# Fused attention and MLP: first tokens normalized in two pairs, a bank of its own for each first sum, and new constants for the instruction plan

## The chip, the cores and the metric

One core of a Trainium2 chip runs the whole kernel. The metric is device microseconds (us) of one execution. The kernel before takes 823.89 us, the median of three runs (822.95 to 825.45). A profiled execution gives a span, 1.8 to 2.0 us shorter than the timed value of the same execution; the accounts below are accounts of spans.

## The reference, cut to what matters

`x` is 2048 x 512, bf16. All three outputs are added.

```python
xn = _layernorm(x, axis=-1)
return x + _A_ref(xn, A_wqkv, A_wo) + _B_ref(xn, B_w1, B_b1, B_w2, B_b2)
# _A_ref: 32 heads of 16
#   p = softmax(q k^T / 4); o = p v; o @ wo
# _B_ref: gelu(layernorm(x) @ w1 + b1) @ w2 + b2, 512 -> 1792 -> 512
```

Attention needs 32 x 2048 x 2048 exponentials, and they decide the time.

## The kernel before

The kernel is a program that plans a program. Each piece of work is added as an operation with an engine, an estimated duration, a priority, its dependences and the PSUM bank that it takes or gives back. A list scheduler simulates the engines with those durations, and the order that it finds becomes the fixed order of instructions on each engine. On the chip every engine works through its list in order and waits by semaphore. So a constant that moves one operation can re-order everything after it; I call each outcome a **plan**.

Queries are worked in groups of 4 heads x 512 queries. For each of 16 key tiles (128 keys) a group needs four **units**: the scores of one head, 128 x 512, in one PSUM bank. ScalarE takes the exponentials of most tiles, two or three units to an instruction. VectorE takes the rest by an int16 bit trick: four conversions from PSUM and four shifted adds for each tile, followed by 20 value products on TensorE where ScalarE's tiles need 4. Value products go into an accumulator bank; at the end of a group the sum is copied out, its denominators travel through DRAM and come back as a broadcast (`rlb`), and VectorE multiplies.

The constants, and the pool of banks for the very first sums:

```python
    early = _Pool([res[7], res[4]])
    wide = _Pool([res[i] for i in (7, 5, 4, 3, 2, 1, 0)])
    T0, KG = 15.0, 15.5
    OUT0, OUT1 = 0.475, 0.25
    OUT, OPEN, RES, RESL, SLK, ALP = 3, 1, 20, 24, 40.0, 25.0
    KTP, QTP = 70.0, 70.0
    HOT = 1
    XACT = 2
    RATE, QO, PO, AO, DO = 23.75, 55.0, 39.5, 25.0, 17.0
```

`OPEN` is how many key tiles may be open for VectorE at once, `RES` how many units must be left in a group for VectorE to be given another of its tiles; `QO`, `AO`, `DO` are offsets of the priorities of query sums, shifted adds and VectorE's value products.

Normalization of four tokens' tiles, with one GpSimd power for all four:

```python
        sl = slice(4 * g, 4 * g + 4)
        ...
        def frs():
            I(nc.gpsimd.tensor_scalar(out=wv1[:, sl], in0=mv[:, sl, 1], scalar1=LN_EPS, ...))
            I(nc.gpsimd.tensor_tensor(out=r1[:, sl], in0=wv1[:, sl], in1=mhalf[:, sl],
                                      op=ALU.pow))
        r = add("POOL", 0.9, frs, [st_op[t] for t in tt] + [mk_half], pr)
        pool = early if g else wide
```

The value products of ScalarE's tile `k` wait for the values of `k`, and also for those of tile `k + 1`; this will matter:

```python
        deps = [unit_exp[g, k, j] for k in ks for j in range(HS)]
        deps += [va_op[k] for k in ks] + [va_op[min(k + 1, NT - 1)] for k in ks]
```

The planner also keeps TensorE's clock up. Where the plan leaves a gap and the last 3.4 us hold less than `NEED` of planned work (in units of 0.215 us), it puts in matmuls of zeros ("fills"):

```python
    NEED = 9.5
    ...
                if (t1 - t0 < 2.0
                        and sum(d for (a, d) in log[-40:] if a > t - 3.4) >= NEED):
                    t += 0.1
                    continue
```

## Time and profile before

| what | us | how to read it |
|---|---|---|
| span of the profiled execution | 820.5 | this execution was timed at 822.46 |
| first exponential | 14.77 | the start: load, normalize, project |
| ScalarE busy from first to last exponential | 777.6 | "work" |
| ScalarE idle in that stretch, before 100 us | 5.8 | "early holes" |
| the same, after 100 us | 10.7 | "late holes" |
| after the last exponential | 11.6 | "tail": last group, output |

These five add up to the span (to rounding), because ScalarE's exponentials run from 14.77 to 808.89. TensorE (94%) and VectorE (90%) are nearly as busy as ScalarE (95%). The lines themselves are in the prediction.

### The profile page before, as it was taken

How to read it: one execution, taken by the hardware profiler on the slowest of the kernel's cores; microseconds unless marked ns; L12 is line 12 of the kernel's file. 1: busy time of each engine (PE TensorE's matmuls, PEld its weight loads, DVE VectorE, ACT ScalarE, POOL GpSimd, SP SyncE). 2: the span in 40 equal slices, each digit the busy share in tenths (PEclk: the TensorE clock that was granted, in tenths of full speed). 3: DMA queues.
4: the chain of work that ended last, by engine and by line, in shares of the span. 5: the costliest groups of instructions: out<-in, count | busy, mean ns of one | idle time of the engine just before them, and what ended most of it. 6: DMA issues, size and time to landing. Idle time of an engine off the chain costs nothing.

```text
span 820.5 us, 22781 instructions
## 1 busy us (share of the span) xinstructions
PE 774.9 (94%) x9671; PEld 256.7 (31%) x9672; DVE 736.4 (90%) x1273; ACT 782.4 (95%) x682; POOL 54.8 (7%) x163
## 2 busy tenths in 40 slices
PE   7999899999999999999999999999999999999997
PEld 3333223333333333233322333323322332333233
DVE  7858999996899998978899998898899999998996
ACT  4899999999999999999999999999999999999994
POOL 2300000000000000000000000000000100000001
PEclk9999999999999999999999999999999999999999
DMA  5400121201100112000001012100001021100010
GB/s 180 116 4 2 34 45 38 49 13 29 29 17 21 48 34 54 27 17 15 9 23 33 30 48 61 28 2 22 22 16 34 27 56 41 29 22 21 4 32 32
DMA packets 54796, 27.96 MB, mean 34 GB/s; under 512 B 40613, under 2 KB 50598, under 8 KB 54690
## 3 DMA queue, kind: packets, MB, share of 16 engines
q1 hardware_dynamic: 52818, 25.03, 11.2%
q8 instruction: 76, 1.25, 0.7%
q10 hardware_dynamic: 1872, 1.44, 0.6%
q14 instruction: 30, 0.25, 0.1%
HBM read 23.85 MB, written 2.61 MB: 32 GB/s over the span
## 4 chain that ended last, share of the span: by engine, by line
PE 38%; DVE 33%; ACT 15%; issue 8%; DMA 6%; POOL 0%; SPq 0%; DVEq 0%; ACTq 0%
ACT p_sb L1197 14%; PE ps L597 14%; DVE x_sb L1274 13%; PE ps L1050 12%; PE ps L1032 11%; DVE tb_x L1299 7%; DVE x_sb L1299 4%; DMA rlb<-rdram 4%; DVE ht L1454 2%; DMA rdram<-rc 1%; DVE stats L719 1%; DVE osb L1333 1%; DVE ont L1347 1%; DVE vs L923 1%; DMA ldram<-osb 1%
## 5 line engine op out<-in xcount | busy, mean ns | idle before, releaser
L1197 ACT ACTIVATE p_sb<-ps 128x1024 bf16<-128x1024 f32 (+1 forms) x656 | 741.6, 1245 | 17.4 <-PE ps L1032 11.5
L1032 PE MATMUL ps<-qz,kt 32*128 32x512 bf16 x2048 | 316.4, 382 | 27.7 <-DVE x_sb L1274 10.5
L1274 DVE TENSOR_SCALAR x_sb<-ps 128x512 int16<-128x512 f32 x440 | 291.6, 683 | 15.4 <-PE ps L1032 14.1
L1299 DVE TENSOR_SCALAR tb_x<-x_sb 128x2048 int16<-128x2048 int16 x293 | 197.0, 684 | 3.5 <-PE ps L1050 2.5
L1032 PEld LDWEIGHTS <-kt 32*128 32x128 bf16 x2048 | 85.5, 91 | 281.1 <-issue 275.0
L1050 PE MATMUL ps<-p_sb,va 128*32 128x512 bf16 x1608 | 158.6, 389 | 0.2 <-DVE x_sb L1274 0.2
L1050 PE MATMUL ps<-tb_x,vs 128*32 128x512 f16 x1172 | 108.5, 382 | 1.1 <-DVE tb_x L1299 0.6
L1299 DVE TENSOR_SCALAR x_sb<-x_sb 128x2048 int16<-128x2048 int16 x147 | 100.4, 683 | 2.8 <-PE ps L1050 2.2
L1050 PEld LDWEIGHTS <-va 128*32 128x32 bf16 x2048 | 48.2, 93 | 109.0 <-issue 106.8
L1050 PEld LDWEIGHTS <-vs 128*32 128x32 bf16 x1760 | 48.1, 95 | 49.1 <-issue 30.5
L1354 POOL TENSOR_SCALAR okt<-lc 128x16 f32<-128x16 f32 x31 | 13.2, 427 | 711.9 <-DMA lc<-ldram 711.9
L597 PE MATMUL ps<-yT,w_r 128*32 128x512 bf16 x896 | 58.6, 381 | 1.3 <-DVE ht L1454 0.6
L597 PE MATMUL ps<-w_sb,ht 128*32 128x512 bf16 x896 | 59.8, 380 | 0.0
L1050 PE MATMUL ps<-x_sb,vs 128*32 128x512 f16 x588 | 57.9, 382 | 1.0 <-DVE x_sb L1299 0.7
L1454 DVE TENSOR_SCALAR ht<-ps,b_sb 128x512 bf16<-128x512 f32 x56 | 41.6, 744 | 6.1 <-PE ps L597 6.1
L1050 PE MATMUL ps<-x_sb,va 128*32 128x512 f16 x440 | 43.3, 383 | 1.2 <-DVE x_sb L1274 0.8
L597 PE MATMUL ps<-wo_pad,ont 128*32 128x512 bf16 x512 | 34.2, 381 | 1.1 <-DVE x_sb L1274 0.6
L597 PEld LDWEIGHTS <-w_r 128*32 128x32 bf16 x896 | 21.6, 96 | 25.3 <-issue 12.1
L1347 DVE TENSOR_TENSOR ont<-osb,rlb 128x512 bf16<-128x512 f32 x31 | 21.3, 687 | 8.4 <-DMA rlb<-rdram 8.4
L1333 DVE COPY osb<-ps 128x512 f32<-128x512 f32 x31 | 21.2, 683 | 8.4 <-PE ps L1050 8.4
L597 PEld LDWEIGHTS <-ht 128*32 128x32 bf16 x896 | 21.7, 96 | 21.1 <-issue 5.9
L1464 ACT ACTIVATE ht<-ht 128x3584 bf16<-128x3584 bf16 x8 | 25.1, 3182 | 0.0
(100 smaller groups left out, 360.2 us busy)
## 6 DMA issues: line engine op xcount, KB each, us to landing
rlb<-rdram SPq DMA_DIRECT2D x31, 256.0 KB
w_r<-in_B_w_dram SPq DMA_DIRECT2D x56, 128.0 KB
x_r<-in_A_x_dram SPq DMA_DIRECT2D x16, 128.0 KB
w_sb<-in_B_w_dram SPq DMA_DIRECT2D x1, 1792.0 KB
out_dram<-ot SPq DMA_DIRECT2D x12, 128.0 KB
x_sb<-in_A_x_dram SPq DMA_DIRECT2D x2, 512.0 KB
wkv<-in_A_wqkv_dram ACTq DMA_DIRECT2D x1, 512.0 KB
x_sb<-in_A_x_dram ACTq DMA_DIRECT2D x1, 512.0 KB
```

Of the source, the lines that this page charges most:

```text
L597: I(nc.tensor.matmul(dst[32 * j:32 * j + 32], lhsT=lhsT[:, 32 * j:32 * j + 32], rhs=rhs, start=start, stop=stop, tile_position=(0, 32 * j)))
L719: I(nc.vector.bn_stats(out=stats[:, t, :], in_=x_sb[:, t, :]))
L1032: I(nc.tensor.matmul(ps[:, bank, :], lhsT=kt[lo:lo + 32, s // 2, k * P:(k + 1) * P], rhs=qz[lo:lo + 32, (qt * NB + s // 2) % NQB, s % 2, : ...
L1050: I(nc.tensor.matmul(ps[32 * j:32 * j + 32, o_bank[g], :], lhsT=vals[:, h * VS:h * VS + 32], rhs=wts(j), start=pv_done[g] == 1, stop=end, ...
L1197: I(nc.scalar.activation(p_sb[:, s0:s1, :].rearrange("p a b -> p (a b)"), ps[:, b0:b0 + n, :].rearrange("p a b -> p (a b)"), AF.Exp, scale ...
L1274: I(nc.vector.tensor_scalar(out=ib[sl][:, j, :], in0=ps[:, pool.bank(key), :], scalar1=LEVEL, scalar2=0.0, op0=ALU.add, op1=ALU.max))
L1299: I(nc.vector.tensor_scalar(out=tb[x % NTB].rearrange("p j q -> p (j q)"), in0=ib[sl].rearrange("p j q -> p (j q)"), scalar1=float(SHIFT[t ...
L1333: e0 = add("DVE", dve(QW), lambda: I(nc.vector.tensor_copy(osb[:, i2, :], ps[:, o_bank[g], :])), pvs + before, pr - 1000, rel=(o_done(g),))
L1347: e4 = add("DVE", dve(QW), lambda: I(nc.vector.tensor_tensor(out=ont[:, slot, :], in0=osb[:, i2, :], in1=rlb[:], op=ALU.mult)), [e3] + lis ...
L1354: I(nc.gpsimd.tensor_scalar(out=okt[:, 0, :], in0=lc[:, i2, :], scalar1=L_MIN, scalar2=None, op0=ALU.is_ge))
L1454: I(nc.vector.tensor_scalar(out=ht[:, fc, :], in0=ps[:, misc.bank(key), :], scalar1=b1_sb[:, fc:fc + 1], scalar2=None, op0=ALU.add))
L1464: I(nc.scalar.activation(out=hv, in_=hv, func=AF.Gelu_apprx_tanh, scale=1.0))
```

## The change

The intent: start the exponentials sooner, give ScalarE less to do, and let the planner keep more VectorE tiles in flight. The diff, cut to its core:

```diff
-    wide = _Pool([res[i] for i in (7, 5, 4, 3, 2, 1, 0)])
+    wide = {key: _Pool([res[i]]) for key, i in (
+        (("xt", 0), 0), (("xt", 1), 1), (("xt", 2), 2), (("xt", 3), 3),
+        (("k", 0, 0), 7), (("k", 0, 1), 7), (("q", 0, 0), 4))}
-    T0, KG = 15.0, 15.5
-    OUT0, OUT1 = 0.475, 0.25
+    T0, NST = 14.0, 12.3
+    KG, R0, VSP, NFI = 15.5, 29.0, 400.0, 2
+    VSE = (5,)
+    OUT0, OUT1 = 0.475, 0.2
-    OUT, OPEN, RES, RESL, SLK, ALP = 3, 1, 20, 24, 40.0, 25.0
-    KTP, QTP = 70.0, 70.0
-    HOT = 1
-    XACT = 2
+    OUT, OPEN, RES, RESL, SLK, ALP = 3, 2, 28, 24, 60.0, 5.0
+    KTP, QTP = 65.0, 75.0
+    HOT = 2
+    XACT = 1
-    RATE, QO, PO, AO, DO = 23.75, 55.0, 39.5, 25.0, 17.0
+    RATE, QO, PO, AO, DO = 23.75, 50.0, 39.5, 30.0, 14.5
...
+        on_act = (0, 1, 3) if g == 0 else (4 * g + 1, 4 * g + 3) if g < XACT else ()
+        for a in range(4 * g, 4 * g + 4, 4 if g else 2):
+            sl = slice(a, a + (4 if g else 2))
+            def frs(sl=sl): ...          # the same two GpSimd instructions, for two tiles
+            r = add("POOL", 1.4, frs, [st_op[t] for t in range(sl.start, sl.stop)] + [mk_half], pr)
...
         va_op[t] = add("DVE", dve(QW), fve, (m, mk_va), pr - 500,
-                       rel=(early.giver(key),))
+                       rel=() if t in VSE else (early.giver(key),))
+        if t in VSE:
+            scaled(early, key, t, va_op[t], pr - VSP)
...
                 o = add("PE", pen(len(rows)), lambda rows=rows: pv(g, k, rows),
-                        deps + [va_op[NT - 1], vs_op[k]], dl + 5.0 - DO, acq=((o_ready, g),),
+                        deps + [va_op[NT - 1] if g > 1 else va_op[k], vs_op[k]], dl + 5.0 - DO, ...
```

Cut away: finer bookkeeping of VectorE's buffers, small changes of other figures of the plan (`HLO`, `DN1`, the lengths of loads), a rule on when an early sum may take the last free bank, and code for VectorE tiles in the first two groups that stays unused (`D1` is empty). I call the lines of `OUT` to `ALP`, of `HOT` and of `RATE` to `DO` the **steady constants** (without `KTP`, `QTP` and `XACT`), as they act in the long middle of the kernel.

## The prediction

> **What bounds the kernel now.** I read the totals first, then a table of stretches, then the waits of the busiest engine, then the first 15 us in order of time. First the profile page's part 1 (busy us, share of the span, instructions):
>
> ```profile
> PE 774.9 (94%) x9671; PEld 256.7 (31%) x9672; DVE 736.4 (90%) x1273; ACT 782.4 (95%) x682; POOL 54.8 (7%) x163
> ```
>
> Three engines are close together, so the shares alone decide nothing. The stretches do (width; busy us of PE, PEld, DVE, ACT, POOL; clock): from the first exponential to 60 us, to 100 us, and to the end of the last exponential at 808.9 us.
>
> ```profile
> 14.77:60.00 45.23, 43.19 (x678) 16.42 (x675) 33.67 (x70) 41.36 (x45) 7.68 (x11) 1.00 0.19 55
> 60.00:100.00 40.00, 36.45 (x446) 11.52 (x442) 34.07 (x59) 38.08 (x38) 2.69 (x8) 1.00 0.07 19
> 100.00:808.90 708.90, 678.47 (x8423) 219.77 (x8416) 652.73 (x1106) 698.17 (x593) 37.92 (x117) 1.00 0.11 29
> ```
>
> Between its first and last exponential (14.77 to 808.9, 794.1 us) ScalarE is busy 41.36 + 38.08 + 698.17 = 777.6 us; it idles 3.9 + 1.9 + 10.7 = 16.5 us. VectorE in the long stretch is at 652.7 / 708.9 = 92%. So ScalarE's stream of exponentials sets the time: start 14.8, work 777.6, holes 16.5, tail 820.5 - 808.9 = 11.6, sum 820.5. The timed median is 823.89, 3.4 above the span; I keep that 3.4. The waits of ScalarE and the groups by shape (busy, mean ns):
>
> ```profile
> ACT p_sb L1197 <- PE ps L1032: 11.5, 30, 1.5
> ACT p_sb L1197 <- PE ps L1050: 2.6, 2, 1.3
> L1197 ACT ACTIVATE p_sb<-ps 128x1536 bf16<-128x1536 f32 x296 | 438.1, 1480 | 9.2 <-PE ps L1032 7.0
> L1197 ACT ACTIVATE p_sb<-ps 128x1024 bf16<-128x1024 f32 x360 | 373.8, 1052 | 8.2 <-PE ps L1032 4.4 <-PE ps L1050 2.6
> L1274 DVE TENSOR_SCALAR x_sb<-ps 128x512 int16<-128x512 f32 x440 | 291.6, 683 | 15.4 <-PE ps L1032 14.1
> ```
>
> The holes are waits for scores (L1032). The means contain overlap with the next instruction: the order of time shows six 1024-wide ones in 5.66 us, so (5.66 - 1.05) / 5 = 0.92 us from start to start; twelve alternating ones take 13.79 us, which leaves (13.7 / 6) - 0.92 = 1.36 us for a 1536-wide one. On VectorE, starts in a dense stretch are 0.60 us apart, both for the 128x512 step from PSUM and the 128x2048 int16 step.
>
> The start, in order of time:
>
> ```profile
> 7.29 1.04 POOL L729 TENSOR_TENSOR r<-wv,mhalf 128x4 f32<-128x4 f32 x1
> 8.37 1.38 DVE L739 TENSOR_SCALAR yT<-x_sb,mv,r 128x512 bf16<-128x512 bf16 x4 [1.48 <-POOL r L729]
> 8.84 1.89 PE L602 MATMUL ps<-ident_bf,yT 128*128 128x128 bf16 x16 [2.29 <-DVE yT L739]
> 10.95 1.56 PE L602 MATMUL ps<-xnT,wq_sb 128*128 128x128 bf16 x16
> 12.55 0.47 ACT L863 ACTIVATE qz<-ps,maskq 128x256 bf16<-128x256 f32 x1 [1.03 <-PE ps L602]
> 13.05 1.14 DVE L856 TENSOR_SCALAR qz<-ps,mask 128x256 bf16<-128x256 f32 x2 [2.02 <-ACT qz L863]
> 14.34 0.40 PE L1032 MATMUL ps<-qz,kt 32*128 32x512 bf16 x4 [0.54 <-DVE qz L856]
> ```
>
> The reader should see a chain: statistics of four token tiles (last at 6.88), one GpSimd power for all four, four normalizations, 16 transposes, 16 query matmuls, scaling, scores. TensorE works without a gap from 8.84 to 12.5, at 118 ns a transpose. The reason is in fine stretches (clock is the column after POOL):
>
> ```profile
> 9.00:9.25 0.25, 0.25 (x5) 0.25 (x4) 0.25 (x2) 0.00 (x0) 0.00 (x0) 0.50 1.10 389
> 12.00:12.25 0.25, 0.25 (x8) 0.25 (x6) 0.00 (x0) 0.00 (x0) 0.00 (x0) 1.00 1.05 319
> ```
>
> **What the Trainium skill says.** "TensorE: Matmul & The Clock Gate", Part 1, section "What's actually happening": half clock is the default, a free-running window of 3413 ns decides, and a 128-column matmul costs about 107 ns cold against 56 ns warm. The trace agrees: the clock is 0.50 from 8.6 to 12.0 (3.4 us), and 16 transposes take 1.89 us. "PSUM — Partial Sum Buffer", section "PSUM bank collisions raise a hardware error": two engines must not be in one bank and quadrant, so a bank is handed over by a semaphore. The trace agrees: the first scores wait for the second L856, which reads bank 0, the bank of the first score, though its result is for the other head. "ScalarE: Activation LUTs", section "What ACT_TABLE_LOAD costs": 186 ns + 0.833 ns per element with immediate operands, about 93 ns of overlap. For 1024 columns that is 1039 ns and 946 from start to start; here 1052 and 922.
>
> **The change, part by part.** Banks, waits and counts are from the two built instruction lists; no time is.
>
> 1. Bank of the query sum. Before, it was in bank 0; now in bank 4, the key sum in 7, transposes in 0 to 3. The first score waits for the 256-column L856 alone: 1.14 - 0.48 = 0.66 us off the start.
>
> 2. Two pairs. The first power waits for two statistics (done 5.30) and not four (6.88): about 5.4 to 6.75, by the 1.35 us that the pair of GpSimd instructions takes now. VectorE still runs all four statistics first, so the first normalization starts at about 6.9 in place of 8.37; the third waits for the second power (8.33), so the last ends at 8.37 + 0.41 + 0.35 = 9.1 in place of 9.75. Three of the four transposes now leave through ScalarE. On TensorE 11 filling matmuls run before the first transpose (14 before), 3 between, 1 more among the query matmuls. If the clock is again half from 8.6 to 12.0: first eight transposes until about 8.0, three fills 8.6, key sum 9.05, eight transposes at 0.113 9.95, eight query matmuls 10.85, a fill 11.3, eight more 12.1. Gain 0.4. The key sum of 384 columns then also delays the key copy; first exponential about 13.6. If the earlier work keeps the clock full: last transposes at 9.4, copied 10.1, query sums 10.4, gain 2.1, first exponential about 12.0. With part 1 the range is 1.1 to 2.8; I take 1.8, as the window's phase is free.
>
> 3. Work moved off ScalarE. The lists hold 357 + 294 exponentials in place of 360 + 296: 12 units of 512, three key tiles, go to VectorE. ScalarE loses 3 x 0.92 + 2 x 1.36 = 5.5 us. Two transposed-token copies in its stream (L758, 0.58 each with overlap, 0.5 net) go too: 1.0. One more copy comes before the stream, where it is part of step 2. Sum -6.5.
>
> 4. Work added. VectorE: 3 x (4 + 4) x 0.60 = 14.4 us, nearly all after 100 us; 652.7 + 14.4 over 708.9 - 6 is 95%. TensorE: 48 matmuls more on shifted values (12 more and 12 fewer on the others cancel), 16 fewer since the fifth key tile's values are scaled from the bank of its first product, 12 fewer fills: +20, at 0.22 us for four about 1 us, beside other work.
>
> 5. Early holes. ScalarE has 1.31 us at 28.2, 0.53 at 31.5, 1.31 at 45.9. The changed order could close some, but puts two 0.6 us copies and four scalings (2.4 us) into VectorE's full stretch from 15 to 30 us. I take -0.5. For the denser VectorE later I take +0.8 of new holes.
>
> Sum: -1.8 - 6.5 - 0.5 + 0.8 = -8.0, so 815.9; I say 815.5, as the other changed constants (more open key tiles, more headroom for the value products) were presumably set to help.
>
> **The rivals.** (a) VectorE becomes the bound: at 95% each late 0.6 us step delays scores or value products, and ScalarE's holes grow by what it was spared. For it: VectorE stood at 96% in 400 to 500 and 600 to 700 us already. Against it: ScalarE idled only about 2% there. Time then 820 to 823. (b) The start's gain is given back: scores start earlier, but keys of tokens 4 to 15 come no sooner, because VectorE is full from 15 to 30 us; ScalarE then waits at 28 us instead of starting late. For it: DVE 4.80, 4.93 and 4.90 of 5 us in those stretches. Against it: 3 us of VectorE idle per 10 us right after. Time about 817.5. (c) Everything helps and the early holes vanish: -2.8 - 6.5 - 3 gives 811.5. A gain over 16.5 us would need more than all of this.
>
> **Range and chances.** (c) and half of (a) bound the range: 810.5 to 820.5. Over 2% faster needs less than 807.4: 0.05. Over 2% slower has nothing for it: 0.01.
>
> **What would show it.** First exponential at 12 to 13.7 us (before 14.77); the first score waiting for a 256-column scaling; clock 0.50 in that stretch or not; ScalarE busy about 776 us in all; VectorE about 751 us, 95% after 100 us; ScalarE's holes between first and last exponential 15 to 18 us; a tail of 11 to 12 us. The prediction is wrong if the holes exceed 20 us (rival a), if holes before 60 us grow past 5 us (rival b), or if the tail moves by over 2 us, for which I gave nothing.

## The result

The kernel after takes 823.96 us (median of 4 runs, 822.69 to 824.75); the kernel before, on the same chip, 824.5 us (4 runs, 822.95 to 825.45). The ratio is 0.9994, with a 95% interval of 0.9972 to 1.0015: the same. A ratio is the mean time of one kernel's fast runs over that of the other's of the same rounds, so not quite the ratio of the medians. The prediction was 815.5 us with a range to 820.5, so the time lies outside it. The spans below differ by +1.5 us where the medians differ by -0.5, because the execution of before that was profiled was a quick one (822.46). So the 3.4 us that the prediction keeps between span and median are 2.0 of the profile's own difference and 1.4 of that quick execution.

Part 1 of the page of the kernel after (busy us, share of the span, instructions):

```profile
PE 770.9 (94%) x9691; PEld 254.2 (31%) x9692; DVE 748.0 (91%) x1298; ACT 776.7 (94%) x676; POOL 53.0 (6%) x165
```

ScalarE is busy 5.7 us less, VectorE 11.6 us more (14.4 was forecast), and TensorE has 20 more matmuls, as counted. The work went where it was meant to go. The same three stretches as before, now from the first exponential at 12.00 us:

```profile
12.00:60.00 48.00, 44.73 (x702) 17.24 (x702) 37.60 (x77) 40.26 (x43) 7.69 (x11) 1.00 0.22 62
60.00:100.00 40.00, 37.69 (x477) 12.51 (x469) 35.38 (x63) 37.39 (x37) 1.83 (x8) 1.00 0.04 12
100.00:812.50 712.50, 675.84 (x8424) 218.71 (x8416) 662.07 (x1124) 693.70 (x589) 36.27 (x117) 1.00 0.11 29
```

ScalarE idles 7.7 us in the first stretch, where it idled 3.9; 2.6 us in the second (1.9); and 712.5 - 693.7 = 18.8 us in the third (10.7). Its work is 40.3 + 37.4 + 693.7 = 771.4 us. The sum for both kernels:

| us | before | after | difference | predicted |
|---|---|---|---|---|
| first exponential | 14.8 | 12.0 | -2.8 | -1.8 |
| work | 777.6 | 771.4 | -6.2 | -6.5 |
| early holes (to 100 us) | 5.8 | 10.4 | +4.6 | -0.5 |
| late holes | 10.7 | 18.8 | +8.1 | +0.8 |
| tail | 11.6 | 9.5 | -2.1 | 0 |
| span | 820.5 | 822.0 | +1.5 | -8.0 |

So 11 us were gained and 12.7 us were lost in holes. The waits of ScalarE in the kernel after (total us, times, longest) and the two shapes of its exponentials:

```profile
ACT p_sb L1237 <- PE ps L1054: 18.1, 40, 2.0
ACT p_sb L1237 <- PE ps L1072: 7.5, 3, 6.3
```

```profile
L1237 ACT ACTIVATE p_sb<-ps 128x1536 bf16<-128x1536 f32 x294 | 433.5, 1474 | 17.2 <-PE ps L1054 14.1 <-PE ps L1072 0.9
L1237 ACT ACTIVATE p_sb<-ps 128x1024 bf16<-128x1024 f32 x357 | 368.8, 1046 | 12.1 <-PE ps L1072 6.6 <-PE ps L1054 4.0 <-ACT p_sb L1237 0.2
```

L1237 is the exponential (L1197 before), L1054 the scores (L1032), L1072 the value products (L1050). The durations of one exponential have not changed. The waits for scores rose from 11.5 to 18.1 us, and there is one wait of 6.3 us for a value product. These are the two losses to explain. Half clock is not the explanation of the late one: after 100 us the profile of the kernel after holds one stretch of it (117.3 to 120.7 us), and ScalarE idles 1.0 us in it and the 1 us behind it.

**The start after.** In order of time (start, us, engine and instruction, idle time before it):

```profile
5.75 0.73 POOL L742 TENSOR_TENSOR r<-wv,mhalf 128x2 f32<-128x2 f32 x1
6.85 0.70 DVE L754 TENSOR_SCALAR yT<-x_sb,mv,r 128x512 bf16<-128x512 bf16 x2
7.29 0.72 PE L602 MATMUL ps<-ident_bf,yT 128*128 128x128 bf16 x8 [1.64 <-DVE yT L754]
...
8.71 0.64 PE L602 MATMUL ps<-ident_bf,yT 128*128 128x128 bf16 x8
...
11.03 1.14 DVE L871 TENSOR_SCALAR qz<-ps,mask 128x256 bf16<-128x256 f32 x2 [1.21 <-ACT qz L878]
11.57 0.40 PE L1054 MATMUL ps<-qz,kt 32*128 32x512 bf16 x4
12.00 1.02 ACT L1237 ACTIVATE p_sb<-ps 128x1024 bf16<-128x1024 f32 x1 [0.34 <-PE ps L1054]
```

The power for two tiles ends at 6.48, the first normalization starts at 6.85, and the first score (11.57) starts while the second scaling, which began at about 11.5, still runs: the bank is no longer in its way. And the clock was full in this start:

```profile
9.00:9.25 0.25, 0.25 (x8) 0.25 (x7) 0.11 (x1) 0.18 (x1) 0.00 (x0) 1.00 1.11 369
```

### The profile page after: what moved, and what is told of

Read it like the earlier page. It is cut to its first block, busy times and chain, and to the rows that moved or that the text cites. A ratio compares the mean times of both kernels' runs of the same rounds, so it can differ in the third digit from the quotient of the medians.

```text
span 822.0 us, 22852 instructions
## 1 busy us (share of the span) xinstructions
PE 770.9 (94%) x9691; PEld 254.2 (31%) x9692; DVE 748.0 (91%) x1298; ACT 776.7 (94%) x676; POOL 53.0 (6%) x165
## 4 chain that ended last, share of the span: by engine, by line
DVE 38%; PE 29%; ACT 16%; issue 9%; DMA 7%; DVEq 0%; SPq 0%; ACTq 0%
ACT p_sb L1237 14%; DVE x_sb L1319 14%; PE ps L597 10%; PE ps L1054 10%; PE ps L1072 9%; DVE tb_x L1343 8%; DMA rlb<-rdram 4%; DVE x_sb L1343 4%; DVE ht L1498 2%; DVE osb L1377 1%; ACT ht L1508 1%; DVE stats L728 1%; DMA rdram<-rc 1%; DVE vs L938 1%; DVE qc L918 1%
## 5 line engine op out<-in xcount | busy, mean ns | idle before, releaser
L1237 ACT ACTIVATE p_sb<-ps 128x1024 bf16<-128x1024 f32 (+1 forms) x651 | 736.0, 1240 | 29.3 <-PE ps L1054 18.1
L1054 PE MATMUL ps<-qz,kt 32*128 32x512 bf16 x2048 | 313.7, 383 | 26.4 <-ACT p_sb L1237 10.9
L1319 DVE TENSOR_SCALAR x_sb<-ps 128x512 int16<-128x512 f32 x452 | 298.1, 679 | 18.2 <-PE ps L1054 16.9
L1343 DVE TENSOR_SCALAR tb_x<-x_sb 128x2048 int16<-128x2048 int16 x302 | 202.1, 681 | 1.8 <-PE ps L1072 0.8
L1054 PEld LDWEIGHTS <-kt 32*128 32x128 bf16 x2048 | 83.4, 91 | 278.9 <-issue 271.9
L1072 PE MATMUL ps<-p_sb,va 128*32 128x512 bf16 x1596 | 156.2, 390 | 1.7 <-DVE osb L1377 0.8
L1072 PE MATMUL ps<-tb_x,vs 128*32 128x512 f16 x1208 | 111.1, 381 | 1.7 <-DVE tb_x L1343 1.4
L1343 DVE TENSOR_SCALAR x_sb<-x_sb 128x2048 int16<-128x2048 int16 x150 | 102.1, 681 | 3.0 <-PE ps L1072 2.8
L1072 PEld LDWEIGHTS <-va 128*32 128x32 bf16 x2048 | 48.9, 93 | 109.0 <-issue 106.3
L1072 PEld LDWEIGHTS <-vs 128*32 128x32 bf16 x1808 | 49.1, 95 | 53.9 <-issue 35.2
L1072 PE MATMUL ps<-x_sb,vs 128*32 128x512 f16 x600 | 58.9, 382 | 1.8 <-DVE x_sb L1343 1.8
L1398 POOL TENSOR_SCALAR okt<-lc 128x16 f32<-128x16 f32 x31 | 10.9, 352 | 712.9 <-DMA lc<-ldram 712.9
L1072 PE MATMUL ps<-x_sb,va 128*32 128x512 f16 x452 | 44.7, 385 | 1.1 <-DVE x_sb L1319 0.9
L1391 DVE TENSOR_TENSOR ont<-osb,rlb 128x512 bf16<-128x512 f32 x31 | 21.2, 684 | 13.7 <-DMA rlb<-rdram 13.7
L597 PEld LDWEIGHTS <-w_r 128*32 128x32 bf16 x896 | 22.8, 96 | 26.2 <-issue 12.1
```

Source lines behind the costliest of these rows:

```text
L597: I(nc.tensor.matmul(dst[32 * j:32 * j + 32], lhsT=lhsT[:, 32 * j:32 * j + 32], rhs=rhs, start=start, stop=stop, tile_position=(0, 32 * j)))
L1054: I(nc.tensor.matmul(ps[:, bank, :], lhsT=kt[lo:lo + 32, s // 2, k * P:(k + 1) * P], rhs=qz[lo:lo + 32, (qt * NB + s // 2) % NQB, s % 2, : ...
L1072: I(nc.tensor.matmul(ps[32 * j:32 * j + 32, o_bank[g], :], lhsT=vals[:, h * VS:h * VS + 32], rhs=wts(j), start=pv_done[g] == 1, stop=end, ...
L1237: I(nc.scalar.activation(p_sb[:, s0:s1, :].rearrange("p a b -> p (a b)"), ps[:, b0:b0 + n, :].rearrange("p a b -> p (a b)"), AF.Exp, scale ...
L1319: I(nc.vector.tensor_scalar(out=ib[sl][:, j, :], in0=ps[:, pool.bank(key), :], scalar1=LEVEL, scalar2=0.0, op0=ALU.add, op1=ALU.max))
L1343: I(nc.vector.tensor_scalar(out=tb[x].rearrange("p j q -> p (j q)"), in0=ib[sl].rearrange("p j q -> p (j q)"), scalar1=float(SHIFT[t]), sc ...
```

## The experiments

Eighteen kernels ran. The accounts first, so that each experiment can be read against the others ("exps by 100" is the busy time of exponentials up to 100 us; "units" are those on VectorE; "ratio" is to the kernel before in the same call, whose medians there were 824.5 to 827.2; the calls ran on several chips; parts of spans are good to 0.1 us):

| run | timed | ratio, 95% | first | work | early holes | late holes | tail | exps by 100 | units |
|---|---|---|---|---|---|---|---|---|---|
| before | 824.5 | | 14.8 | 777.6 | 5.8 | 10.7 | 11.6 | 78.8 | 440 |
| after | 824.0 | 0.9994 (0.9972-1.0015) | 12.0 | 771.4 | 10.4 | 18.8 | 9.5 | 77.7 | 452 |
| e1 | 823.1 | 0.9962 (0.9913-1.0011) | 11.9 | 777.6 | 10.4 | 12.5 | 9.2 | 76.8 | 440 |
| e2 | 835.1 | 1.0104 (1.0060-1.0148) | 13.5 | 778.9 | 10.2 | 19.7 | 10.7 | 76.3 | 440 |
| e3 | 823.3 | 0.9958 (0.9913-1.0004) | 11.8 | 775.1 | 10.5 | 12.5 | 11.0 | 77.7 | 444 |
| e4 | 836.1 | 1.0121 (1.0076-1.0166) | 13.8 | 782.4 | 5.5 | 20.7 | 9.4 | | 432 |
| e5, wrong result | 834.8 | 1.0115 (1.0088-1.0143) | 11.9 | 773.1 | 12.0 | 27.1 | 9.5 | | 452 |
| e6 | 829.2 | 1.0048 (1.0011-1.0086) | 12.0 | 772.4 | 10.2 | 22.4 | 9.5 | 77.8 | 452 |
| e7 | **818.2** | 0.9920 (0.9896-0.9944) | 12.0 | 777.7 | 9.4 | 8.4 | 9.2 | 77.8 | 440 |
| e8 | 830.7 | 1.0084 (1.0045-1.0122) | 11.8 | 776.0 | 7.8 | 22.1 | 9.1 | 80.4 | 444 |
| e9 | 823.1 | 0.9956 (0.9895-1.0016) | 13.8 | 777.8 | 5.4 | 9.8 | 11.7 | 80.1 | 440 |
| e10 | 826.0 | 0.9980 (0.9920-1.0040) | 12.0 | 773.6 | 10.2 | 19.5 | 9.5 | | 452 |
| e11 | 827.2 | 1.0012 (0.9949-1.0074) | 12.0 | 779.3 | 9.8 | 13.5 | 10.0 | 78.2 | 436 |
| e12 | 831.0 | 1.0052 (0.9987-1.0116) | 12.0 | 770.6 | 9.2 | 22.1 | 14.1 | 78.0 | 452 |
| e13 | 825.3 | 1.0027 (0.9984-1.0069) | 12.0 | 779.5 | 3.1 | 12.1 | 15.1 | 84.0 | 436 |
| e14 | 836.5 | 1.0160 (1.0123-1.0197) | 12.0 | 774.8 | 9.2 | 21.5 | 16.2 | 78.0 | 448 |
| e15 | 825.9 | 1.0018 (0.9993-1.0044) | 11.9 | 778.7 | 9.4 | 12.7 | 9.3 | 77.9 | 440 |
| e16 | 830.7 | 1.0061 (0.9981-1.0142) | 11.8 | 779.0 | 9.4 | 17.7 | 10.6 | | 440 |
| e17 | 829.0 | 1.0022 (0.9947-1.0096) | 11.8 | 776.5 | 9.2 | 16.8 | 13.3 | | 444 |
| e18 | 825.2 | 0.9974 (0.9902-1.0047) | 13.7 | 778.0 | 9.3 | 13.3 | 9.5 | | 440 |

The holes of each kernel are those of one profiled execution, and executions of one plan differ: the kernel before took 822.6 to 834.6 us in these calls, the quick ones at a mean granted clock of 0.998, the two slowest at 0.978 and 0.981. So a difference of a few us of holes between two profiles need not be the plan's.

### e1: the start alone

The kernel before with the banks, the pairs, the third copy on ScalarE, and the planner's figures for the start; everything later as before.

```diff
-    wide = _Pool([res[i] for i in (7, 5, 4, 3, 2, 1, 0)])
+    wide = {key: _Pool([res[i]]) for key, i in (...)}      # as in the change
-    T0, KG = 15.0, 15.5
+    T0, KG = 14.0, 15.5
+        for a in range(4 * g, 4 * g + 4, 4 if g else 2):  # pairs, as in the change
```

> The kernel before with the start of the change alone (two pairs, first sums in banks 0 to 3, 7 and 4, three first copies on ScalarE, start time and load estimates); exponential counts stay 360 + 296. If the start gain is real and is only lost by what else the change does: first exponential at 12.0 us (before 14.77), time 2 to 3 us under before. Rival, keys come no sooner so the gain is given back: first exponential at 12.0, but the hole near 28 us grows from 1.3 to about 4 us, time as before.

The first exponential comes at 11.9 us, as after. Yet 76.8 us of exponentials are done by 100 us, against 78.8 before (80.1 in e9 below, where the start of before ran at full clock). The start's 2.8 us are given back, and 2 more, before 100 us, as rival (b) said; not in a hole near 28 us, as expected, but in two of 2.7 and 3.6 us that end at 45 and 64 us, both waits for value products. (e1 ran at half clock from 88.1 to 91.5 us; e7 below, the same plan without that, has 77.8.) With nothing but the start changed, the late holes and the time are near those of before.

### e2: the second query sum later

The hole of 6.34 us in the kernel after, in order of time:

```profile
25.34 1.05 PE L597 MATMUL ps<-xnT,wq_sb 128*32 128x512 bf16 x16
...
28.15 1.05 PE L597 MATMUL ps<-wkv,xnT 128*32 128x512 bf16 x16 [0.90 <-DVE qc L918]
...
30.08 1.25 DVE L956 CAST va<-ps 128x512 bf16<-128x512 f32 x2
...
30.69 0.40 PE L1072 MATMUL ps<-p_sb,va 128*32 128x512 bf16 x4
...
31.18 2.85 ACT L1237 ACTIVATE p_sb<-ps 128x1024 bf16<-128x1024 f32 x3 [6.34 <-PE ps L1072]
```

ScalarE waits for room in `p_sb`, the ring of finished exponentials. The room comes when a value product (30.69) has read it; that one waits for values of token tile 4 (30.08), which wait for their sum (28.15). Ahead of that sum in TensorE's order stands the second query sum (25.34). In the kernel before, that sum ran at 36.45 us. e2 puts it 10 us later in the plan of the kernel after:

```diff
-         m = project(misc, key, pr, pr + 22, ...
+         m = project(misc, key, pr, pr + (32 if n == 1 else 22), ...
```

> The changed kernel, with the second query projection not planned before 31 us, as it was before (in the changed kernel it stands ahead of the value products of tile 4). Theory: it holds TensorE, bank 7 and VectorE in front of the value product that frees the exponentials' slots, and is the cause of the 6.3 us hole at 25 to 31 us; the hole falls to 3 us or less and the time by 3 us. Rival, VectorE's full queue of statistics and normalizations delays the fourth tile's values anyhow: hole 5 us or more, time as the changed kernel.

The early holes stayed at 10.2 us, and exponentials done by 100 us at 76.3. The hole itself was 4.6 us, between what the theory (3 or less) and its rival (5 or more) had said; but the exponentials began 1.5 us later here (13.5), and the hole ended at 31.6 us, much as in the kernel after (31.2). So moving the query sum did not bring the room sooner. The test is not clean, since e2 ran at half clock from 24.3 to 27.7 us, just in front; the theory finds no support, and is not strictly refuted. The edit also re-planned the rest: VectorE lost its 12 extra units, and the kernel took 835.1 us. That was the first sign of how far a small edit reaches.

### e3 and e4: the plan's figure for the broadcast

VectorE waited for the broadcast `rlb` 13.7 us in the kernel after and 8.4 us in the kernel before. VectorE's waits in the kernel after, from 100 us on:

```profile
DVE x_sb L1319 <- PE ps L1054: 16.9, 24, 1.9
DVE ont L1391 <- DMA rlb<-rdram: 13.7, 10, 2.5
```

and in the kernel before:

```profile
DVE x_sb L1274 <- PE ps L1032: 14.1, 24, 1.7
...
DVE ont L1347 <- DMA rlb<-rdram: 8.4, 10, 2.2
```

The planner assumes 2.2 us for that transfer; the traces show 4.6 to 5.3 us. One of the ten waits and what it does to ScalarE, in order of time, kernel after:

```profile
321.12 0.69 DVE L1391 TENSOR_TENSOR ont<-osb,rlb 128x512 bf16<-128x512 f32 x1 [1.73 <-DMA rlb<-rdram]
...
322.53 0.37 PE L1054 MATMUL ps<-qz,kt 32*128 32x512 bf16 x1 [1.30 <-DVE ht L1498]
...
324.60 2.37 ACT L1237 ACTIVATE p_sb<-ps 128x1536 bf16<-128x1536 f32 x2 [1.56 <-PE ps L1054]
```

VectorE waits 1.73 us for the transfer; TensorE's next score waits 1.30 us for a bank that VectorE frees; the scores behind it come late; ScalarE idles 1.56 us. e3 (after) and e4 (before) plan the transfer at 5.5 us:

```diff
-                 [e3, last_rlb[0]], pr - 500, lat=2.2)
+                 [e3, last_rlb[0]], pr - 500, lat=5.5)
```

> The changed kernel, with the plan's estimate for the last DMA of the sums (broadcast of the reciprocals) raised from 2.2 to 5.5 us, so that the product waiting for it stands later in VectorE's order. Theory: VectorE waiting in order for that DMA (13.7 us in all) makes ScalarE's late holes; waits fall under 4 us, ScalarE's holes after 100 us from 18.8 to about 11, time 6 us lower. Rival, the density of VectorE (95%) makes the holes: waits fall, holes stay above 16 us, time as the changed kernel.

> The kernel before with the same estimate raised. Its waits for that DMA are 8.4 us, ScalarE's holes after 100 us 10.7. Theory: waits under 3, holes 6 to 8, time 2 to 4 us lower less what 2 key tiles fewer on VectorE (432 units in place of 440) cost ScalarE, some 3.7 us: so -1 to +2. Rival, density: no fewer holes, time 3 to 4 us higher.

VectorE's wait for `rlb` nearly vanished in both (1.1 and 0.5 us). In e3 the late holes fell from 18.8 to 12.5, though with 8 units fewer on VectorE; in e4 they rose from 10.7 to 20.7. So the removed wait does not fix the holes by itself. But e4 also ran at half clock for 41 us of its late stretch (mean granted clock 0.969 to 0.975 in its four runs), and 10.1 of its 20.7 us of idle time lie there or in the 1 us behind, so e4 does not tell the wait from the clock. The time of e3 is that of before.

### e5 and e10: the waiting product held back

To take the wait away without a new plan, I let the planner work as before and wrote the product (`ont<-osb,rlb`) five VectorE instructions further down the list.

```diff
-            [e3] + list(ont_use.get(g - NON, ())), pr)
+            [e3] + list(ont_use.get(g - NON, ())), pr, late=5)
```

> The changed kernel with only the 31 products that wait for the broadcast DMA moved five VectorE instructions later; the plan, the counts (357 + 294) and every other order stay. Theory: VectorE's waits for that DMA fall from 13.7 to under 3 us, ScalarE's holes after 100 us from 18.8 to 11 to 13, time 5 to 7 us under the changed kernel (about 818). Rival, density of VectorE makes the holes: holes stay above 17, time as the changed kernel.

e5 gave a wrong result: some products were, as I take it, written after the matmuls that read them (e10 rules this out, and is right). It shows nothing about the theory, save that the edit was bad. e10 writes a product out at the latest before its first reader, and has e6's fills (below) so that it is to be compared with e6:

> e6 (changed kernel with raised fills: 829.2, holes after 100 us 22.4, VectorE's waits for the broadcast DMA 16.5) with the 31 products moved up to five VectorE instructions later, mended so that each still stands ahead of its readers. Theory of the DMA wait: waits under 4 us, holes 12 to 15, time about 820. Rival, density: holes stay above 19, time within 2 us of e6.

Its result is right. The wait for `rlb` is 0 where e6 had 16.5 us, and the order is otherwise e6's. The late holes went from 22.4 to 19.5 and the time from 829.2 to 826.0. So this wait costs about 3 us of holes in this pair of profiles; the times are not clear of noise (824.6 to 827.2 against 825.5 to 830.3). The chain shown above is real, but it is not the main loss: VectorE's wait for scores rose instead (17.2 to 23.3 us), and the expected 12 to 15 us of holes did not come.

### e6, e7 and e9: more fills

Some runs showed half clock in the middle of the kernel. In e1, from 721 us on:

```profile
721.23 0.40 PE L1593 MATMUL ps<-ones_bf,zeros_bf 128*32 128x512 bf16 x4
722.75 0.38 PE L1039 MATMUL ps<-qz,kt 32*128 32x512 bf16 x1 [1.12 <-DVE x_sb L1281]
723.06 0.62 PE L1593 MATMUL ps<-ones_bf,zeros_bf 128*32 128x512 bf16 x4
```

The same four fills take 0.40 us at 721 and 0.62 us at 723, with one wait of 1.12 us between. The stretch at half clock lasted to about 733 us, 10 us. To keep it out without another order, I raised the fill threshold; nothing but fills is added (264 after 15 us in e1, 672 in e7).

```diff
-    NEED = 9.5
+    NEED = 12
```

e6 is the kernel after with this, e7 is e1 with this, e9 is the kernel before with this.

> The changed kernel with the threshold for filling matmuls raised from 9.5 to 12 (684 against 300 rows of them after the start), nothing else reordered. Theory of the clock: half-clock stretches (one at 116 to 122 us in the changed kernel's profile) vanish and with them about 2 us of holes; run to run spread shrinks; time 1 to 2 us lower. Rival: the fills delay scores and time is the same or up to 3 us higher.

> The kernel before with the start alone (as e1) and the raised fill threshold. e1 had half clock at 720 to 736 us and at 88 to 92 us in its profile, with holes of 5.0 us in its last stretch and 8.2 from 40 to 100 us. If the clock took what the start gave: no half-clock stretch after the start, last stretch's hole about 1 us, holes 40 to 100 us about 4, time 6 to 8 us under e1's 823.1. Rival, holes are the plan's: time within 2 us of e1.

> The kernel before with only the raised fill threshold. It separates the clock from the start in e7 (818.2). If e7's gain is the start's 2.8 us plus the clock: this runs at 820.5 to 822, first exponential near 14.5, holes after 100 us 9 to 11. Rival, the fills made all of e7's gain: about 818. Rival, fills cost as in e6: 826 to 829.

e7 takes 818.16 us (817.72 to 818.52), 0.8% below the kernel before, at full clock in the profile from the start up to 814.0 us: it beats both kernels. Against e1 its late holes fell from 12.5 to 8.4 (3.1 us of e1's lie in its half-clock stretch or the 1 us behind) and the time by 5 us, though the two intervals overlap. The kernel before gained little from the same edit (823.1, interval across 1), and the kernel after did not gain (829.2, its interval just touching that of the kernel after). So fills explain none of what the kernel after lost. Nor do they always keep the clock up: after 100 us and before the tail, the profiles of e6, e11 and e12 hold 6.8, 3.4 and 20.4 us of half clock, those of e7 and e9 none.

### e8 and e13: without the wait for the next tile's values

```diff
-        deps += [va_op[k] for k in ks] + [va_op[min(k + 1, NT - 1)] for k in ks]
+        deps += [va_op[k] for k in ks]
```

Correctness needs only the values of tile `k` itself. e8 is the kernel after with this edit, e13 is e7 with it.

> The changed kernel without the dependence of a value product on the next tile's values (not needed: each tile's rows are padded), which makes the product of tile 3 wait for tile 4. Theory: the slots of the exponentials come free without tile 4, the 6.3 us hole at 25 to 31 us vanishes (holes to 40 us under 3). Its plan puts 444 units on VectorE in place of 452, 4 us more work on ScalarE: net time 0 to 2 us lower. Rival, VectorE's queue there is the cause: hole stays above 4 us, time 4 us higher.

> e7 (818.2: start alone, more fills) without the wait of a value product for the next tile's values. Exponentials' busy time by 100 us is 78.8 in the kernel before, 77.7 in the changed one, 77.8 in e7, but 80.4 in e8, the only one without that wait. If that wait gives the start's gain back at each change of token group: by 100 us 80 or more, holes from 40 to 100 us under 4 (7.2 in e7); 436 units on VectorE in place of 440 cost 2 us; time 816 to 818. Rival, supply of keys is the limit: by 100 us under 78.5, time 820.

The exponentials' busy time up to 100 us (width; busy; clock) in the kernel after:

```profile
11.50:100.00 88.50, 77.65 (x79) 1.00 0.14 41
```

and in e13:

```profile
11.50:100.00 88.50, 84.04 (x84) 1.00 0.16 45
```

ScalarE's waits for value products up to 100 us, in the kernel after, in e7 and in e8 (e13 has none):

```profile
ACT p_sb L1237 <- PE ps L1072: 6.3, 1, 6.3
```

```profile
ACT p_sb L1204 <- PE ps L1057: 7.4, 3, 3.6
```

```profile
ACT p_sb L1237 <- PE ps L1072: 2.8, 1, 2.8
```

In e13 ScalarE is ahead of e7 by 84.0 - 77.8 = 6.2 us at 100 us, and its early holes are 3.1 instead of 9.4. In e8 it is ahead of the kernel after by 2.7 us, and early holes fell from 10.4 to 7.8; the hole of 6.3 us is gone, and one of 2.8 us ends at 43.5 us. So the planned wait on the next tile's values is what gave the start's gain back: in the plan of e7 that is shown; in the kernel after it is 2.6 of the 4.6 us that early holes had grown by. But the lead did not reach the end. e13 lost it in a new plan (late holes 12.1 against 8.4, tail 15.1 against 9.2, 4 units fewer on VectorE) and took 825.3; e8 took 830.7.

### e11 and e12: early part and steady constants crossed

With e6 and e7 these make a square, all with the raised fill threshold. e11 is the kernel after with the steady constants of before (what else the change did, `KTP`, `HLO` and the new rules too, stays), e12 is e7 with those of after.

```diff
# e12; e11 is the reverse, in the kernel after
-    OUT, OPEN, RES, RESL, SLK, ALP = 3, 1, 20, 24, 40.0, 25.0
-    HOT = 1
-    RATE, QO, PO, AO, DO = 23.75, 55.0, 39.5, 25.0, 17.0
+    OUT, OPEN, RES, RESL, SLK, ALP = 3, 2, 28, 24, 60.0, 5.0
+    HOT = 2
+    RATE, QO, PO, AO, DO = 23.75, 50.0, 39.5, 30.0, 14.5
```

> e6 with the constants of the steady part (open key tiles, reserves, headroom, priorities of scores and terms) as in the kernel before: 436 units on VectorE in place of 452, ScalarE's work 7 to 8 us more (about 780). If those constants make the late holes: holes after 100 us fall from 22.4 to 8 to 12, time 822 to 825. Rival, the early part of the change throws the later plan off: holes stay about 20, time 835.

> e7 (818.2; holes after 100 us 8.4) with the steady part's constants of the changed kernel: 357 + 294 exponentials and 452 units on VectorE, as there, so ScalarE's work 772, 5.5 us less than e7. If a denser VectorE (by 12 units) makes late holes by itself: holes 18 to 22, time 822 to 828. If the units are free and the holes came from elsewhere in the change: holes 8 to 11, time 812 to 815.

With the constants of before the late holes are 8.4 (e7) and 13.5 (e11), with those of after 22.1 (e12) and 22.4 (e6). The work is 777.7 and 779.3 against 770.6 and 772.4. In this square the steady constants spare ScalarE about 7 us of work and give it 9 to 14 us more of idle time. Half clock takes part in this, but cannot make it all: of the late holes, 4.5 us in e12, 3.2 in e6 and 1.4 in e11 lie in half-clock stretches or the 1 us behind, none in e7.

### e14 and e15: the steady constants split

```diff
# e14, from e7
-    OUT, OPEN, RES, RESL, SLK, ALP = 3, 1, 20, 24, 40.0, 25.0
+    OUT, OPEN, RES, RESL, SLK, ALP = 3, 2, 28, 24, 40.0, 25.0
# e15, from e7
-    RATE, QO, PO, AO, DO = 23.75, 55.0, 39.5, 25.0, 17.0
+    RATE, QO, PO, AO, DO = 23.75, 50.0, 39.5, 30.0, 14.5
```

> e7 with two of the steady constants of the changed kernel (open key tiles 2, reserve 28): 448 units on VectorE in place of 440, priorities as in e7. e7's holes after 100 us are 8.4, e12's (all constants, 452 units) 22.1. If units on VectorE make the holes: 15 or more, work about 773, time 821 to 825. If the priorities do: holes 8 to 11, time 814 to 816.

> e7 with the other steady constants of the changed kernel (headroom of scores 50, of value products 30, of terms 14.5); units stay 440, so work stays 777.7. If these priorities make the holes: 15 or more after 100 us, time 824 or more. If the units do: holes 8 to 11, time 817 to 820.

Two open tiles and the larger reserve alone (448 units on VectorE) give 21.5 us of late holes and a tail of 16.2; the priorities alone, with 440 units, 12.7 us and 9.3. By then the constants for open tiles looked guilty. But each of these is one plan.

### e16, e17 and e18: the same constants, other plans

I moved the planned time of the output projection (`OUT0`), which belongs to neither theory: in e7 to 0.485 (e16), in e12 to 0.465 (e17) and 0.445 (e18).

```diff
-    OUT0, OUT1 = 0.475, 0.25
+    OUT0, OUT1 = 0.485, 0.25
```

> The start alone with the raised fill threshold (818.2 us, holes after 100 us 8.4, tail 9.2), with one neutral edit: the planned time of the output projection inside a token group is moved from 0.475 to 0.485 of the group, 0.2 us. The plan is reordered in its second half (968 of some 2400 VectorE rows), the count of units on VectorE stays 440. Theory 1 (the steady constants themselves cost the late holes): 816 to 821 us, late holes 7 to 11 us, tail 9 to 11 us. Theory 2 (any reordering scatters the holes, and the fast plan was luck): 822 us or more, late holes over 12 us or a tail over 12 us.

> The start and fills with the steady constants of the kernel after (831.0 us, 452 units on VectorE, late holes 22.1, tail 14.1), with the same kind of neutral edit (0.475 to 0.465), which here reorders most of the plan and leaves about 448 units on VectorE. Theory 1: late holes stay at 18 to 25 us, time 826 to 834. Theory 2: late holes anywhere from 8 to 25; under 13 would speak for luck.

> As the run before, with 0.475 to 0.445, which leaves about 436 units on VectorE, fewer than the 440 of the kernel before, under the steady constants of the kernel after. If the number of units on VectorE makes the late holes: about 8 to 12 us. If the constants make them by the order of the tiles, whatever the number: 16 to 25 us. If it is luck: anything. ScalarE's work 778 to 780 us in all cases.

e16 has e7's constants and e7's 440 units, and takes 830.7 us instead of 818.2. Up to 500 us the two agree: ScalarE idles 14.2 us in e7 and 14.0 in e16. Then, from 500 to 700 us, in e7:

```profile
500.00:700.00 200.00, 195.93 (x2444) 62.71 (x2441) 183.56 (x312) 198.12 (x170) 8.08 (x32) 1.00 0.10 28
```

and in e16:

```profile
500.00:700.00 200.00, 189.33 (x2233) 58.92 (x2233) 180.03 (x304) 189.63 (x162) 12.11 (x33) 0.98 0.08 22
```

ScalarE (the fourth busy time) idles 1.9 us in the one and 10.4 us in the other, where a part also ran at half clock (0.98 on average). An edit of about 0.25 us in a planned time, neutral as to both theories, cost 9.3 us of late holes, more than the 8.1 us that the kernel after had lost. Of these, 4.4 us lie in the two half-clock stretches or the 1 us behind each; but a run of e16 at a mean clock of 0.997, which leaves room for some 5 us of half clock in all (an estimate: twice 0.003 of the span), still took 829.3 us, against 818.5 at 0.998 in e7. So the time follows the plan, and not the clock of that one profile. Theory 2 of the expectation holds for e16. e17 (444 units, not the 448 that I had expected) and e18 (440, not 436) lie at 16.8 and 13.3, both below what theory 1, the constants, had said (18 to 25 and 16 to 25). As e18 came out with 440 units, fewer units than before were not tested; it has e7's load under the new constants, and its 13.3 us lie between e7's 8.4 and e16's 17.7. The six kernels with the old steady constants (before, e1, e7, e9, e11, e16; four plans, as e9 and e7 add only fills) have late holes of 8.4 to 17.7, mean 12.1; the six correct ones with the new (after, e6, e10, e12, e17, e18; four plans likewise) 13.3 to 22.4, mean 18.8; runs that change other waits or figures of the plan are left out. The two ranges overlap.

## Why the prediction was wrong

**Bank of the query sum and pairs (steps 1 and 2): right.** The step took 1.8 us out of a range of 1.1 to 2.8, "as the window's phase is free". The measured pair of profiles shows 2.8, but that pair mixes phases: before had half clock, after had full. Other runs show the missing corners. The start of before at full clock is e9's:

```profile
13.77 1.02 ACT L1197 ACTIVATE p_sb<-ps 128x1024 bf16<-128x1024 f32 x1 [1.10 <-PE ps L1032]
```

and e18 has the new start at half clock, with its first exponential at 13.65 ("about 13.6" was the prediction for that branch):

```profile
9.00:9.25 0.25, 0.25 (x2) 0.00 (x0) 0.00 (x0) 0.00 (x0) 0.00 (x0) 0.50 1.10 356
```

So the change gains 13.77 - 12.00 = 1.8 us at full clock and 14.77 - 13.65 = 1.1 us at half.

**Work off ScalarE and work added (steps 3 and 4): right.** ScalarE's work fell by 6.2 us (said 6.5), its busy total is 776.7 (776), VectorE's 748.0 (751), and TensorE has the 20 more matmuls. VectorE's share after 100 us is 662.1 / 712.5 = 93%, not 95%, since its work there grew by 9.3 us and not 14.4, and the stretch did not get shorter.

**Early holes (step 5): wrong, by 5.1 us.** The step said "The changed order could close some [...] I take -0.5". Early holes grew by 4.6 us, and with them the start's gain was gone: rival (b), named and passed over. Its reason, keys that come no sooner, was not the one: e13 has 84.0 us of exponentials by 100 us, so keys would have allowed more. The wait that ends last was not seen: value products in the plan wait for the next tile's values, and the ring of exponentials then stays full. In e13, without that dependence, ScalarE is 6.2 us further at 100 us than in e7. In the kernel after the waits for value products to 100 us rose from 2.6 to 6.3 us, 3.7 of the 4.6. I had read the waits for scores in this stretch and had not followed the waits for value products, of which the view of before already showed 2.6 us.

**Late holes (step 5): wrong, by 7.3 us, the larger half.** The step said "For the denser VectorE later I take +0.8 of new holes". It treated holes as a small term that grows with VectorE's load. The runs show something else: with three engines at 90% or more, each waiting in order for the others, the holes depend on the plan and not on the load alone. One neutral edit moved them from 8.4 to 17.7 us at the same load (e16). The kernel before, with 10.7, is near the low end of these plans, so a change that re-plans it has more to lose than to gain. That re-planning alone can bring new holes of this size is shown by one pair, e7 and e16; that it did so in the kernel after is not. Whether the new constants add to it is suggested by the means (12.1 and 18.8) and by fewer units going with smaller holes (13.3, 16.8, 22.1 for 440, 444 and 452 units in e18, e17 and e12; e8, with 444 units and other waits, has 22.1), but not settled. How the 8.1 us divide stays open. Rival (a) was nearest in time, 820 to 823, for a reason that holds in part: VectorE, at 93%, was not shown to be the bound, but work spared and holes gained nearly cancel. Work plus late holes is 788.3 before, 790.2 after and 792.7 in e12.

One link inside these holes is measured: VectorE's wait for the broadcast costs about 3 us (e10 against e6, one profile each). The remainder, as I read the waits, is mutual waiting of VectorE for scores and TensorE for banks; that is not shown, as no run takes it away alone.

**Tail: wrong, by 2.1 us, in the good direction.** The prediction gave 0. e1 and e7 have the same shorter tail (9.2) without any of the later changes, so it seems to come with the start and the plan that follows from it; no run takes it apart. Plans e12 to e14 and e17 have 13 to 16 us. Why is open.

**The constants "were presumably set to help"**: the prediction rounded down for this. No run supports it; taken alone, e14 and e15 were both slower than e7 (836.5 and 825.9 against 818.2 us).

All three conditions under which the prediction called itself wrong were met: holes of 29.2 us in all (limit 20), of 7.7 us before 60 us (limit 5), and a tail moved by over 2 us.

## What to carry to other kernels

Where a planner writes fixed orders for several engines that are each over 90% busy, do not predict the idle time of a new plan from the old plan's: build a few neutral variants and see how far they scatter before crediting or blaming a constant. An earlier start is worth only what the next wait downstream leaves of it, so follow that wait (here for room, through a value product, to values not yet needed) before counting the gain. Test each part alone: the start with more fills, without the new constants, was the best version at 818.2 us. That time, too, is partly luck: an edit of about 0.25 us in its plan made it 830.7 (e16).

## What the Trainium skill lacked or had wrong

- "TensorE: Matmul & The Clock Gate", section "Why this matters for your kernels", advises no idle gaps of TensorE beyond about 3 us to avoid drops in the middle of a kernel. Here the clock fell to half after much shorter gaps: in e1 at 723 us the longest wait just before was 1.12 us (TensorE busy 1.98 of the 3.4 us from 719.6), and in the kernel after, which ran partly at half clock between 116 and 122 us, 1.35 us (TensorE busy 2.60 of the 4 us from 112 to 116). So this advice alone is too lax here. The page's section "A second HAM failure mode: psum-queue depth-cycling" does tell of half clock from frequent short idles, without a length for them.
- The same page, Part 1, "What's actually happening", puts the ramp's penalty below 1% of a span. That held for the start (about 1.0 us between e9's and before's first exponential). It does not cover half clock re-entered in mid-kernel, which other sections of the page treat: in e4, with 41 us of it after 100 us, ScalarE idled 10.1 us in or just behind these stretches (1.2% of the span), which is no measure of what the clock alone cost.
- No page that I looked up gives the time of a GpSimd power: 0.73 us for 128 x 2 elements, 1.04 us for 128 x 4.
- "DMA: Bandwidth & Descriptors", section "Anatomy of one DMA — SWDGE (gpsimd) path", gives a fit of 2.0 us plus the bytes over 436 GB/s, measured on another kind of queue than the one used here. For the 256 KB of the broadcast out of DRAM that would be an estimate of 2.6 us; it took 4.6 to 5.3 us in the kernels before and after. With the plan's 2.2 us for it VectorE waited 8.4 us in the kernel before, with 5.5 us in the plan 0.5 us (e4).
